# Sliding-window attention and a squared-ReLU feed-forward in one kernel: the second group's up-projection moved ahead of the first group's down-projection, and all nine groups' down-projections by seven products

## The chip, the cores and the metric

The kernel runs on one core of a Trainium2 chip. The metric is the device time of one execution, in microseconds (us). The core's engines run side by side, each through its own list of instructions in order: TensorE (PE, with its weight loads PEld), VectorE (DVE), ScalarE (ACT), GpSimd (POOL) and SyncE (SP). Here POOL issues the loads that convert float32 to bfloat16 on the way in, and SP issues transposes by DMA and most stores.

## The reference

Attention over 8 batches, 8 heads, 576 positions of 64 numbers each, with a causal window of 128 and a linear bias by distance, and then a feed-forward over all 4608 tokens.

```python
def _attn_ref(q, k, v):
    B, H, S, D = q.shape                       # 8, 8, 576, 64
    scores = (1 / sqrt(D)) * np.matmul(q, k.transpose(0, 1, 3, 2))
    rel = pos[:, None] - pos[None, :]
    slopes = 2.0 ** (-8.0 * (np.arange(H) + 1) / H)
    bias = slopes[:, None, None] * (-np.abs(rel))[None]
    mask = (rel >= 0) & (rel < 128)
    scores = np.where(mask, scores + bias, -1e9)
    attn = softmax(scores)
    return np.matmul(attn, v)

def _moe_ref(x, w_in, w_out):                  # x 4608 x 512, w_in 512 x 2048, w_out 2048 x 512
    r = np.maximum(x @ w_in, 0.0)
    return (r * r) @ w_out
```

All inputs and the output are float32; the kernel computes in bfloat16 with float32 sums.

## The kernel before

The tokens are worked in blocks of 128 positions of one batch (the last block of a batch has 64, and two such are paired). The 40 blocks are numbered 0 to 39 in the order in which they are taken; four of them make a group of 512 tokens, and there are nine groups, 0 to 8.

**Attention of a block.** POOL loads its k, q and v (tasks `lkq8`, `lv8`; lines L590 and L597). For blocks 0 to 7 PE transposes k and q through an identity matrix (`tp4.0`, `tp4.1`, L653) and ACT or DVE copies the result out (`ev4.0.0`); from block 8 on SP transposes by DMA (`kqT8`, L638). PE multiplies the scores (`s8`, L711) into four PSUM banks, ACT takes the exponentials (`e8.0` to `e8.3`, L734, 128x512 each), DVE multiplies by the window's mask (`m8.0` to `m8.3`, L742, L745, L749, 128x512 each), PE multiplies by v in two halves (`pv8.0`, `pv8.1`, L816), and DVE normalises (`r8.0`, `n8.0`, L832, L845). Blocks 0 to 3 have no earlier keys: there the bias is written by PE from the tables `slopes` (`b0`, L764), and no mask is needed. The block's result is transposed into `xT` (`xp4` by PE, L865, or `x8` by SP).

**Block 0** has a way in of its own: its k and q come as float32 by four loads on SP's and ACT's queues (`lk0.0`, `lk0.1`, `lq0.0`, `lq0.1`, L572) and DVE casts them (`ck0`, `cq0`, L441).

**Up-projection.** Groups 0 to 2 go plainly: `u0.r.e` is one piece of a group's product with `w_in` (L965), then ReLU by ACT (`reluu...`, L932) and the square (`squ...`). Groups 3 to 8 use seven half-size products in place of eight (`f3.u.p`, L1059), with sums by DVE (`us`, `ut`, `c11.g.u` and so on) and snapshots out of PSUM (`s1.g.u` and so on).

**Down-projection.** The constant `G_STR = 1` says from which group on the seven products are used. Group 0 goes plainly: 16 pieces `o0.t.part` of four matmuls 128x512 each (L1137), copied out by ACT (`oe0...`). Groups 1 to 8 use products `p1.p.z`: p is 1 to 7, z the half, eight matmuls 128x256 each (L1221). These need, for each group, eight DVE sums of 128x1024 (`S1` to `S4`, L1367), four snapshots out of PSUM (`s1_1`, `s5_1`, `s2_1`, `s3_1`, L443), three additions by DVE (`c11_1`, `c22_1`, `c12_1`), and the sums of `w_out` in `wsum` (`ws`, L1179, eight in all, used by every group). One product in progress holds up to three PSUM banks, where a plain piece holds one of the eight.

**Loads of the weights.** `w_in` comes in five pieces (`w_in0` and `w_in1` of 256 KB, the others of 512 KB), `w_out` in four of 512 KB, all by POOL (L535, L538), between the loads of blocks 3 to 7.

**The order** is written out by hand in the string `ORDER`: each engine takes its own tasks in the order in which they stand there; the letter behind the colon names the engine (a ACT, d DVE, g POOL, s SP, none PE), the numbers behind it the PSUM banks or buffers. Costs and due times in the code only check and place that order; the order itself decides what is queued behind what. The piece `fill` (L420) adds idle matmuls of 128x128 (L422) where the planner sees PE wait in the first 30 us.

Of the kernel before, what the change touches and what calls it, by code (L numbers as in the profile page):

```python
# [8 lines left out]
FP32 = mybir.dt.float32  # L9
# [8 lines left out]
N_HW = 1  # L18
N_PE = 8
# [11 lines left out]
IOTA = 3  # L31
# [5 lines left out]
G_STR = 1  # L37
# [19 lines left out]
lk0.0:s iota:g ident:d dist1:d slope1.0:d slope0.3:d one0.1:d lk0.1:a lkq2:g warm0:d slope1.1:d warm::0 lkq1:g  # L57
lq0.0:s slope1.3:a slope1.2:a slope0.2:a ck0:d slope0.0:a slope0.1:a lq0.1:a one0.2:d tp0.0::1 tp2.0::2 tp2.1::3
ev2.0.0:d ev2.1.0:d tp1.0::4 ev1.0.0:a tp1.1::5 b2::6,7 s2 ev1.1.0:a b1::0,2 s1 b0::3,4 e2.0:a e2.1:a e1.0:a
e1.1:a ev0.0.0:a cq0:d tp0.1::5 lv2:g pv2.0::6 r2.0:d ev0.1.0:d lv1:g lkq3:g lv0:g w_in0:g w_in1:g w_in2:g lv3:g  # L60
w_in3:g w_out0:g lkq4:g w_in4:g w_out1:g w_out2:g lkq5:g lv4:g pv1.0::7 pv1.1::0 pv2.1::2 r1.1:d r1.0:d n1.0:d
s0 tp3.0::5 tp3.1::1 n1.1:d e0.0:a b3::7,0 ev3.1.0:a ev3.0.0:a xp1.0::3 s3 n2.0:d r2.1:d one0.0:d pv0.0::6
n2.1:d e0.1:a pv0.1::1 x1.0:a xp2.0::2 one0.3:d r0.0:d x2.0:a u0.1.0::5 r0.1:d n0.0:d n0.1:d xp0.0::4 u0.2.0::3
e3.0:a e3.1:a x0.0:d dist0:d u0.0.1::6 u0.0.0::2 pv3.0::1 pv3.1::7 one1.4:d r3.0:d n3.0:d r3.1:d one1.1:d n3.1:d
u0.1.1::0 u0.0.2::4 xp3.0::1 u0.2.1::7 x3.0:d mask1.2:a reluu0.1.1:a:0 reluu0.0.1:a:1 reluu0.2.0:a:2 squ0.0.1:d
squ0.2.0:d u0.3.0::0 reluu0.1.0:a:3 u0.2.2::6 reluu0.2.1:a:1 mask0.3:a reluu0.0.2:a:2 squ0.2.1:d reluu0.2.2:a:1
squ0.2.2:d squ0.1.0:d u0.3.1::3 w_out3:g o0.2.0::1 tp4.0::5 tp4.1::7 squ0.1.1:d one1.7:d ev4.1.0:d squ0.0.2:d
reluu0.3.0:a:1 mask1.5:a mask0.5:a mask1.6:a mask0.6:a reluu0.0.0:a:3 ev4.0.0:a one1.3:d squ0.0.0:d u0.1.2::4
reluu0.1.2:a:0 reluu0.3.1:a:2 us3.0:d one1.0:d u0.0.3::6 reluu0.0.3:a:3 one1.8:d u0.3.2::0 s4::2,7,5,4 mask0.2:a
mask1.3:a mask0.4:a mask0.0:a mask1.0:a e4.0:a e4.3:a squ0.1.2:d squ0.0.3:d mask0.1:a mask1.7:a mask1.1:a  # L70
mask0.7:a reluu0.3.2:a:0 squ0.3.0:d squ0.3.2:d u0.2.3::3 reluu0.2.3:a:3 mask1.4:a one1.6:d squ0.2.3:d e4.1:a
u0.1.3::6 reluu0.1.3:a:1 squ0.1.3:d lkq6:g u0.0.4::2 e4.2:a o0.2.1 u0.3.3::4 o0.1.0::0 o0.1.1 o0.1.2 ws0.0:d
one1.2:d m4.3:d one1.5:d reluu0.0.4:a:0 us1.0:d m4.1:d m4.2:d tp5.0::3 tp5.1::7 lkq7:g lv5:g lv7:g lv6:g lkq8:g
lkq9:g lv8:g m4.0:d pv4.0::6 r4.0:d pv4.1::5 n4.0:d r4.1:d n4.1:d ev5.0.0:a o0.2.2 ev5.1.0:a reluu0.3.3:a:3
s5::2,3,7,6 e5.0:a e5.3:a e5.1:a e5.2:a xp4.0::4 o0.1.3 o0.2.3 tp6.0::5 tp6.1::2 lkq10:g ev6.0.0:a oe0.1.0:a:0
oe0.2.0:a:1 o0.3.0::6 tp7.0::3 tp7.1::7 st0.1.0:s lkq11:g ws0.1:d ws1.0:d x4.0:d us3.1:d us2.0:d squ0.3.3:d
m5.0:d m5.1:d ev6.1.0:d s6::4,5,2,0 e6.0:a e6.1:a e6.2:a e6.3:a ev7.1.0:a kqT8:s lv9:g kqT9:s squ0.0.4:d
ev7.0.0:d m5.3:d m5.2:d zerov10:d zerokqT10:d us0.0:d lv10:g zerov11:d o0.0.0::1 pv5.1::3 pv5.0::4 m6.0:d m6.1:d
o0.0.1 o0.0.2 kqT10:s zerokqT11:d r5.1:d r5.0:d n5.0:d n5.1:d m6.2:d squ0.3.1:d m6.3:d ws1.2:d s7::5,2,0,7
e7.0:a pv6.0::4 xp5.0::3 x5.0:a o0.0.3 pv6.1::5 e7.2:a e7.3:a e7.1:a oe0.0.0:a:2 m7.3:d m7.1:d r6.0:d m7.0:d  # L80
r6.1:d m7.2:d kqT11:s u1.0.0::3 u1.0.2::0 u1.0.3::7 pv7.0::2 pv7.1::1 r7.0:d r7.1:d n6.0:d n7.0:d n7.1:d
reluu1.0.0:a:1 reluu1.0.3:a:3 squ1.0.3:a n6.1:d o0.3.1 u1.0.7::3 reluu1.0.2:a:0 xp7.0::7 s8::4,2,0,1 xp6.0::5
lkq12:g lv12:g lkq13:g lv13:g lkq14:g o0.3.2 e8.0:a e8.3:a reluu1.0.7:a:2 e8.2:a squ1.0.0:d us2.1:d us2.3:d
x7.0:d x6.0:d ws1.1:d ws0.3:d m8.3:d m8.2:d o0.3.3 oe0.3.0:a:3 u1.1.1::7 u1.1.2::4 m8.0:d e8.1:a m8.1:d ws1.3:d
pv8.1::5 u1.0.1::1 u1.1.4::3 r8.1:d reluu1.1.2:a:3 reluu1.1.1:a:1 squ1.1.1:d pv8.0::0 r8.0:d n8.0:d squ1.0.2:d
reluu1.0.1:a:1 squ1.0.1:a n8.1:d s9::6,2,4,7 e9.0:a e9.1:a squ1.0.7:d squ1.1.2:d kqT12:s x8:s u1.0.6::1 e9.3:a
reluu1.0.6:a:1 e9.2:a m9.0:d m9.1:d m9.3:d ws0.2:d m9.2:d p1.1.0::0 u1.0.4::6 u1.0.5::5 reluu1.0.4:a:0
reluu1.1.4:a:2 s10::2,7,1,4 pv9.1::6 pv9.0::3 p1.1.1 r9.0:d r9.1:d n9.0:d e10.0:a n9.1:d squ1.0.4:d
reluu1.0.5:a:3 e10.3:a m10.3:d squ1.0.5:d us3.3:d m10.0:d s1_1:d:4 u1.1.5::2 u1.1.0::5 lkq15:g lv14:g lv11:g
lkq16:g x9:s e10.2:a e10.1:a reluu1.1.5:a:0 squ1.1.5:a s12::3,4,6,1 e12.0:a squ1.1.4:a e12.3:a st0.2.0:s kqT13:s  # L90
kqT14:s kqT16:s kqT15:s squ1.0.6:d m10.2:d u1.1.6::7 p1.2.0::2 u1.1.7::3 m12.0:d m10.1:d e12.2:a m12.2:d m12.3:d
p1.2.1 c11_1:d pv10.0::1 reluu1.1.7:a:3 reluu1.1.0:a:0 squ1.1.0:d e12.1:a reluu1.1.6:a:1 squ1.1.6:a pv12.1::6
pv10.1::3 pv11.0::5 m12.1:d r11.0:d squ1.1.7:a n11.0:d u1.1.3::4 pv11.1::2 pv12.0::7 u2.0.0::5 reluu2.0.0:a:2
reluu1.1.3:a:0 r10.0:d r11.1:d n11.1:d r10.1:d n10.0:d r12.1:d u2.0.5::2 u2.0.1::1 reluu2.0.5:a:1 n10.1:d
r12.0:d n12.0:d n12.1:d S1.1.0:d S3.1.0:d squ1.1.3:a s13::3,5,7,4 e13.0:a e13.1:a e13.3:a S1.1.1:d S2.1.0:d
S2.1.1:d S4.1.1:d S3.1.1:d u2.0.7::6 u2.0.6::2 squ2.0.5:a reluu2.0.6:a:3 e13.2:a reluu2.0.7:a:0 m13.3:d lv16:g
lkq17:g lkq20:g x12:s x10:s x11:s u2.0.4::3 p1.5.0::5 reluu2.0.4:a:1 p1.5.1 s14::4,2,7,6 s5_1:a:5 e14.0:a
# [232 lines left out]
def kernel(  # L330
# [1099 lines left out]
```

## Time and profile before

| | |
|---|---|
| time, median of 3 runs | 295.23 us (293.89, 295.23, 295.64) |
| the profiled execution: its time, its span | 293.89 us, 292.1 us |
| PE busy, matmuls | 282.8 us (97%), 3443 |
| DVE busy, instructions | 247.1 us (85%), 645 |
| ACT busy, instructions | 226.9 us (78%), 445 |
| POOL busy | 106.5 us (36%) |
| granted TensorE clock | 1.00 |
| plain down-projection, L1137 | 64 matmuls 128x512, 25.9 to 58 us |
| seven products, L1221 | 880 matmuls 128x256, from 63 us on |

The span runs from the first to the last instruction; 1.8 us of the execution's time lie around it. A matmul's duration in the profile is longer than the distance to the next one, because matmuls overlap in the array; what counts for a queue of them is the distance from start to start. The same holds, less strongly, for DVE and ACT. Where the timeline merges n alike instructions, that distance is the merged time less one duration, divided by n - 1.

### The profile page before, as it was taken

The numbers are of one execution on the slowest core, as the hardware profiler recorded it, in microseconds if no ns is written. First come the engines' busy times: TensorE is split into PE (matmuls) and PEld (weight loads), VectorE is DVE, ScalarE is ACT, GpSimd is POOL, SyncE is SP. The second block draws the span as 40 slices with busy tenths as digits, with TensorE's granted clock in tenths as the row PEclk, the third lists the DMA queues.
The fourth block names the chain that finished last, engine by engine and source line by source line (L and its number), as shares of the span: only waits on it lengthen the run. The fifth ranks groups of instructions, "written<-read, shape, count | busy, mean of one in ns | idle before, by whom it ended". The sixth has DMA issues, their size and how long they took to land.

```text
span 292.1 us, 8683 instructions
## 1 busy us (share of the span) xinstructions
PE 282.8 (97%) x3443; PEld 238.5 (82%) x3443; DVE 247.1 (85%) x645; ACT 226.9 (78%) x445; POOL 106.5 (36%) x132
## 2 busy tenths in 40 slices
PE   5889999999999999999999999999999999999994
PEld 2589766788888888888888888888898888888884
DVE  4444588877798699999999999999999898999883
ACT  3658967688789695899999999899886957858710
POOL 8954377393265372912573630820000000000000
PEclk9999999999999999999999999999999999999999
DMA  9999999999999999999999999998500523010225
GB/s 124 166 199 195 190 167 179 145 130 141 180 167 143 179 207 171 131 139 173 185 173 141 142 197 154 168 168 139 116 3 5 152 80 91 1 41 20 90 81 154
DMA packets 170921, 39.64 MB, mean 136 GB/s; under 512 B 156928, under 2 KB 170368, under 8 KB 170880
## 3 DMA queue, kind: packets, MB, share of 16 engines
q0 software_dynamic: 115184, 18.10, 95.1%
q1 hardware_dynamic: 54800, 20.26, 37.6%
q10 hardware_dynamic: 896, 0.72, 1.0%
q8 instruction: 27, 0.44, 0.6%
q14 instruction: 14, 0.11, 0.1%
HBM read 36.70 MB, written 9.44 MB: 158 GB/s over the span
## 4 chain that ended last, share of the span: by engine, by line
PE 87%; DMA 8%; POOL 4%; issue 0%; ACT 0%; DVE 0%; POOLq 0%
PE o L1221 33%; PE h L1059 26%; PE h L965 13%; PE pv L816 6%; PE s L711 5%; DMA vf<-in_v_dram 3%; DMA kqT<-kq 3%; PE o L1137 2%; DMA kq<-in_q_dram 2%; POOL kq L590 2%; POOL vf L597 1%; POOL w_in_sb L535 1%; PE o L1323 1%; PE xp L865 0%; PE tp L653 0%
## 5 line engine op out<-in xcount | busy, mean ns | idle before, releaser
L734 ACT ACTIVATE P<-s 128x512 bf16<-128x512 f32 x120 | 65.6, 612 | 5.2 <-PE s L711 4.9
L1221 PEld LDWEIGHTS <-g 128*128 128x128 bf16 x624 | 60.0, 98 | 7.0
L590 POOL DMA_DIRECT2D kq<-in_k_dram x39 | 33.9, 868 | 69.4 <-DMA kqT<-kq 65.6
L932 ACT ACTIVATE rt<-h 128x512 bf16<-128x512 f32 (+1 forms) x73 | 42.3, 600 | 14.7 <-PE h L965 9.9
L1080 DVE TENSOR_TENSOR rt<-h,f 128x512 bf16<-128x512 f32 x72 | 48.7, 686 | 4.1 <-PE h L1059 1.3
L924 ACT ACTIVATE g<-rt 128x512 bf16<-128x512 bf16 x80 | 48.9, 636 | 1.4 <-DVE rt L1085 0.7
L1221 PE MATMUL o<-w_out_sb,g 128*128 128x256 bf16 x384 | 47.7, 273 | 0.0
L965 PE MATMUL h<-xT,w_in_sb 128*128 128x128 bf16 (+1 forms) x512 | 46.4, 246 | 0.0
L443 ACT ACTIVATE f<-h 128x512 f32<-128x512 f32 x59 | 34.9, 606 | 11.1 <-PE h L1059 10.9
L965 PEld LDWEIGHTS <-w_in_sb 128*128 128x128 bf16 x512 | 38.9, 98 | 3.9
L1059 PE MATMUL h<-xT,w_in_sb 128*128 128x256 bf16 x288 | 41.4, 273 | 0.1
L1059 PEld LDWEIGHTS <-w_in_sb 128*128 128x128 bf16 x384 | 35.8, 98 | 5.2 <-issue 0.3
L742 DVE TENSOR_TENSOR P<-P,masks 128x512 bf16<-128x512 bf16 x96 | 37.1, 420 | 2.2 <-ACT P L734 2.1
L597 POOL DMA_DIRECT2D vt<-in_v_dram x36 | 30.8, 876 | 16.6 <-PE pv L816 9.0
L590 POOL DMA_DIRECT2D kq<-in_q_dram x39 | 33.7, 865 | 5.7 <-DMA w_out_sb<-in_moe_w_out_dram 2.3
L926 DVE TENSOR_TENSOR g<-rt 128x512 bf16<-128x512 bf16 (+1 forms) x65 | 26.1, 415 | 6.9 <-ACT rt L932 6.6
L845 DVE TENSOR_TENSOR x<-pv,rec 128x256 bf16<-128x256 f32 (+1 forms) x80 | 31.4, 414 | 0.5
L1221 PE MATMUL o<-wsum,sums 128*128 128x256 bf16 x256 | 31.7, 273 | 0.0
L1221 PE MATMUL o<-wsum,g 128*128 128x256 bf16 x240 | 30.5, 273 | 0.0
L1059 PEld LDWEIGHTS <-us 128*128 128x128 bf16 x288 | 27.1, 98 | 3.7
L1087 ACT ACTIVATE rt<-rt 128x512 bf16<-128x512 bf16 x38 | 24.1, 637 | 5.6 <-DVE rt L1080 5.2
L816 PEld LDWEIGHTS <-P 128*128 128x128 bf16 (+1 forms) x576 | 24.0, 100 | 5.0 <-issue 2.3
(81 smaller groups left out, 398.3 us busy)
## 6 DMA issues: line engine op xcount, KB each, us to landing
out_dram<-f SPq DMA_DIRECT2D x54, 128.0 KB, 2.6
kq<-in_k_dram POOLq DMA_DIRECT2D x31, 128.0 KB, 5.9
kq<-in_q_dram POOLq DMA_DIRECT2D x31, 128.0 KB, 6.5
vt<-in_v_dram POOLq DMA_DIRECT2D x28, 128.0 KB, 7.0
w_out_sb<-in_moe_w_out_dram POOLq DMA_DIRECT2D x4, 512.0 KB, 14.5
w_in_sb<-in_moe_w_in_dram POOLq DMA_DIRECT2D x3, 512.0 KB, 10.2
out_dram<-f SPq DMA_DIRECT2D x4, 256.0 KB, 5.0
out_dram<-f SPq DMA_DIRECT2D x13, 64.0 KB, 2.1
```

The source lines that it names most:

```text
L443: nc.scalar.activation(o, i, AF.Copy)
L590: nc.gpsimd.dma_start(view(kq[s_kq[m].idx], i), source(src, m, split))
L597: nc.gpsimd.dma_start(tile_of(s_v[m])[0:n, :, 0:D], source(v, m))
L734: nc.scalar.activation(flat(Pt[sP.idx]), sS[i].tile.rearrange("p (j t) -> p j t", j=2)[:, :, lo:hi], AF.Exp, bias=0.0, scale=scale)
L742: nc.vector.tensor_tensor(flat(Pt[sP.idx]), flat(Pt[sP.idx]), flat(masks), op=ALU.mult)
L816: nc.tensor.matmul(sv.tile[0:n, hi * (D + 1):(hi + 1) * (D + 1)], prob, tile_of(s_v[mk])[:, h, 0:D + 1], start=mk == parts[0][1], stop=mk ...
L924: nc.scalar.activation(o, i, AF.Square, bias=0.0, scale=1.0)
L932: nc.scalar.activation(rts[srt.idx][:, 0:n], slot.tile[:, 0:n], AF.Relu, bias=0.0, scale=1.0)
L965: nc.tensor.matmul(slot.tile[:, f * w:(f + 1) * w], w_in_sb[:, cc, fc * 128:(fc + 1) * 128], xT[:, cc, lo % (XR * 128):lo % (XR * 128) + w ...
L1059: nc.tensor.matmul(slot.tile[:, j * 256:j * 256 + 256], a, b_, start=fresh and j == 0 and c == 0, stop=c == 1, skip_group_check=True)
L1080: nc.vector.tensor_tensor(rts[srt.idx], slot.tile, other(), op=ALU.add)
L1221: nc.tensor.matmul(slot.tile[:, z * 256:z * 256 + 256], stationary(c), moving(c), start=fresh and z == 0 and c == 0, stop=c == F - 1, skip ...
```

## The change

It has four parts, and the order is written anew around them.

1. `G_STR = 0`: group 0's down-projection also goes by seven products. The 64 matmuls of 128x512 go, and 112 of 128x256 come; with them eight sums `S1.0.0` to `S4.0.1`, the additions `c11_0`, `c22_0`, `c12_0` and four snapshots come, and the four copies `oe0` go.
2. The order: group 1's up-projection (`u1`) stands ahead of group 0's down-projection, and the pieces of `w_out` are loaded later. All pieces of `w_in` and the loads of blocks 3 to 6 now stand ahead of `w_out0`, and `w_out3` comes behind the loads of blocks 8, 9 and 10.
3. `HWK = True`: block 0's q comes by POOL (`lq0`), converted on the way, in place of the two loads on SP's and ACT's queues and the cast `cq0`. POOL's first five tasks are loads of k and q, and `iota`, which makes the numbers for the identity matrix and the bias, is the sixth. `TABLE = True` adds one tiny exponential on ACT at the start (`table`).
4. `MASK2 = True`: a mask product covers four heads in place of two, 128x1024 in place of 128x512, so two in a block in place of four. It waits for two exponentials in place of one. The values' half `pv` waits for two exponentials in both kernels.

```diff
+SPLIT = False
+HWK = True
+MASK2 = True
+TABLE = True
...
-G_STR = 1
+G_STR = 0
...
+    def touch():
+        nc.scalar.activation(scratch, warm[:, 0:1], AF.Exp, bias=0.0, scale=1.0)
+    if TABLE:
+        plan.add({"ACT": 1400.0}, EARLY, touch, [t_wz], name="table")
...
-            for i, src in enumerate((k, q)):
+            for i, src in enumerate((k, q)[:1 if HWK else 2]):
...
+            if HWK:
+                l_q = plan.add({"POOL": 890.0}, key, lambda: nc.gpsimd.dma_start(view(kq[s_kq[m].idx], 1, False),
+                                                                               source(q, m)), [], [s_kq[m]],
+                               dma=ns, name=f"lq{m}")
+                c_k = plan.add(engs, key, lambda: cast_kq(0), t_l[0:2], [], [s_st], name=f"ck{m}", after=l_q)
+                t_kq[m] = [c_k, l_q]
...
-            t_P.append(plan.add({"DVE": dve(cols, 2)}, due - 31 + i, mask,
-                                [t_e] + t_mask[1] + (t_mask[0] if kind != "diag" else []), name=f"m{ms[0]}.{i}"))
+        for i in range(2 if MASK2 else 4):
+            nh = 4 if MASK2 else 2
+            t_P.append(plan.add({"DVE": dve(cols * nh // 2, 2)}, due - 31 + i,
+                                lambda i=i, nh=nh: mask(slice(nh * i, nh * i + nh)),
+                                t_es[nh // 2 * i:nh // 2 * (i + 1)] + t_mask[1] + (t_mask[0] if kind != "diag" else []),
+                                name=f"m{ms[0]}.{i}"))
```

Out of the two orders, PE's tasks where the parts change places, and POOL's and DVE's first tasks:

```
PE before:   ... u0.3.1 o0.2.0 tp4.0 ... u0.3.3 o0.1.0 o0.1.1 o0.1.2 tp5.0 ... o0.0.3 pv6.1 u1.0.0 u1.0.2 ... u1.1.3 pv11.1 pv12.0 u2.0.0 ...
PE after:    ... u0.3.3 xp5.0 s7 pv6.1 u1.0.6 ... u1.1.5 u1.1.7 p0.1.0 p0.1.1 s8 u1.1.6 p0.5.0 u1.1.3 p0.2.0 u1.1.4 p0.2.1 s9 ...
             p0.7.0 p1.2.0 s12 p0.7.1 p1.1.0 p1.1.1 p1.2.1 pv11.1 pv11.0 p0.4.0 pv10.1 pv12.1 pv12.0 p0.4.1 u2.0.3 ...
POOL before: iota lkq2 lkq1 lv2 lv1 lkq3 lv0 w_in0 w_in1 w_in2 lv3 w_in3 w_out0 lkq4 w_in4 w_out1 w_out2 lkq5 lv4 w_out3 lkq6 ...
POOL after:  lk1 lk2 lq1 lq0 lq2 iota lv1 lv2 lk3 lq3 lv0 w_in1 w_in0 w_in2 lv3 w_in3 lk4 lq4 lk5 lq5 lk6 w_in4 lq6 lv4 lk7 lq7
             lv5 lv6 w_out0 lv7 w_out1 lkq9 lkq8 w_out2 lkq10 lv8 w_out3 lkq11 ...
DVE before:  ident dist1 slope1.0 slope0.3 one0.1 warm0 slope1.1 ck0 ...
DVE after:   warm0 one0.0 one0.1 ident ev1.0.0 ck0 dist1 slope1.0 slope1.1 slope0.3 ev0.1.0 ...
```

Over the whole of both orders the tasks that differ in number are these; besides, 64 tasks (copies out of PSUM, ReLUs, squares, snapshots) go from ACT to DVE and 49 from DVE to ACT.

| engine | task | before | after |
|---|---|---|---|
| PE | plain pieces `o0` (4 matmuls 128x512) | 16 | 0 |
| PE | products `p` (8 matmuls 128x256) | 112 | 126 |
| DVE | mask products | 120 of 128x512 | 60 of 128x1024 |
| DVE | sums `S` (128x1024) | 64 | 72 |
| DVE | additions `c..` of the down-projection | 24 | 27 |
| DVE | snapshots of both projections | 17 | 18 |
| DVE | copies `ev` out of PSUM | 6 | 13 |
| DVE | ReLUs in place, squares of sums (`reluc`, `sqc`, `sqf`) | 34, 24, 6 | 38, 27, 7 |
| ACT | copies `ev` and `oe` | 14 | 3 |
| ACT | ReLUs in place, squares of sums | 38, 66 | 34, 62 |

More of the change, by code (lines that the diff above doesn't have):

```diff
@@ L56 @@
 ORDER = """
[L57 to L61, printed above, removed]
@@ new lines @@
+m6.1:d u0.3.3::0 n6.0:d xp5.0::5 x5.0:d x4.0:a reluu0.0.4:a:0 s7::7,2,3,1 reluu0.3.3:a:2 e7.0:a e7.3:a e7.2:a
+e7.1:a pv6.1::4 w_out0:g lv7:g w_out1:g lkq9:g lkq8:g w_out2:g lkq10:g u1.0.6::0 u1.0.2::5 kqT9:s us3.0:d
+squ0.0.4:d squ0.2.3:d r6.1:d n6.1:d squ0.3.2:d xp6.0::7 u1.0.3::1 u1.0.0::4 zerokqT10:d m7.0:d x6.0:a m7.1:d
+pv7.1::3 reluu0.1.3:a:0 squ0.1.3:d r7.1:d pv7.0::2 kqT8:s reluu1.0.3:a:1 u1.0.5::7 u1.0.4::6 r7.0:d n7.0:d
+n7.1:d xp7.0::1 x7.0:d u1.0.1::2 lv8:g w_out3:g lkq11:g lv9:g kqT10:s lkq12:g lv12:g lkq13:g lv13:g squ1.0.3:a
@@ L245 @@
     SELF = {"ACT": 120.0, "DVE": 110.0}
-    BEGIN = {"POOL": 840.0, "SP": 740.0, "ACT": 740.0, "DVE": 860.0, "PE": 1190.0}
+    BEGIN = {"POOL": 700.0, "SP": 740.0, "ACT": 740.0, "DVE": 700.0, "PE": 1190.0}
     FIRST = {"POOL": 1100.0, "SP": 1150.0, "ACT": 1150.0}
@@ L407 @@
     xt = ring("x", size["x"], [128, d_model])
-    stages = [wsum.rearrange("p s c t -> p (s c t)")[:, 0:4 * d_model].bitcast(FP32)]
-    plan = Plan({"b": 8, "f": NF, "rt": RT, **{f"g{f}.{t}": 2 for f in range(FCB) for t in range(2)}, "rec": 4, "ut": UT, "s1": 1, "s2": 1, **{f"v0.{i}": 1 for i in range(L)}, "kqT0": L, "stage": 2, **size})
+    stages = [x.rearrange("p c t -> p (c t)").bitcast(FP32) for x in (wsum[:, i] for i in range(4))]
+    plan = Plan({"b": 8, "f": NF, "rt": RT, **{f"g{f}.{t}": 2 for f in range(FCB) for t in range(2)}, "rec": 4, "ut": UT, "s1": 1, "s2": 1, **{f"stage{i}": 1 for i in range(4)}, **{f"v0.{i}": 1 for i in range(L)}, "kqT0": L, **size})
     def bank(slot, name):
@@ L662, in evac @@
                     o = tile_of(sT)[:, i * C + c0:i * C + c1, 0:n]
-                    if split:
+                    if split and not (HWK and i):
                         src = st.tile[:, 0:512].rearrange("p (i g c) -> p c g i", i=4, c=C)[:, c0:c1]
@@ L669, in transpose_kq @@
                 w = (c1 - c0) * n
-                evs[i].append(plan.add({"ACT": act(w), "DVE": dve_p(w, 1 if split else 2)}, due - 58, evac,
+                evs[i].append(plan.add({"ACT": act(w), "DVE": dve_p(w, 1 if split and not (HWK and i) else 2)}, due - 58, evac,
                                        [t_tp[i]], [], [st], name=f"ev{m}.{i}.{c0}"))
@@ new lines, in flat, with mask @@
+        def flat(t, w):
+            return t[:, w].rearrange("p j t q -> p j (t q)")[:, :, lo:hi]
+        def mask(w):
+            nh = w.stop - w.start
+            if kind == "full":
+                nc.vector.tensor_tensor(flat(Pt[sP.idx], w), flat(Pt[sP.idx], w), flat(masks, w), op=ALU.mult)
+            elif kind == "diag":
+                pt = Pt[sP.idx][:, w]
+                nc.vector.tensor_tensor(pt, pt, masks[:, w, 1:2, :].to_broadcast([128, nh, 2, 128]), op=ALU.mult)
+            else:
+                pt = Pt[sP.idx][:, w].rearrange("p j t (i q) -> p (j t) i q", i=2)
+                mk = masks[:, w].rearrange("p j t (i q) -> p (j t) i q", i=2)[:, :, 0:1, :]
+                nc.vector.tensor_tensor(pt, pt, mk.to_broadcast([128, 2 * nh, 2, 64]), op=ALU.mult)
@@ new lines, in job, with expo @@
+        t_es = []
+        for i in range(4):
+            def expo(i=i):
+                nc.scalar.activation(flat(Pt[sP.idx], slice(2 * i, 2 * i + 2)),
+                                     sS[i].tile.rearrange("p (j t) -> p j t", j=2)[:, :, lo:hi],
+                                     AF.Exp, bias=0.0, scale=scale)
+            t_es.append(plan.add({"ACT": act(cols)}, due - 31 + i, expo, [t_s[i // 2], t_e0], [] if i else [sP],
+                                 [sS[i]], name=f"e{ms[0]}.{i}"))
+            t_e0 = t_e0 or t_es[0]
@@ L821, in values @@
             t_pv = plan.add({"PE": 4 * len(parts) * 30.0 + 30}, due - 12 + hf, pv,
[L822 removed]
+                            (t_P[hf:hf + 1] if kind == "lone" else t_P[len(t_P) // 2 * hf:len(t_P) // 2 * (hf + 1)]) + [x for _, mk in parts for x in t_v[mk]],
                             [sv], rel, name=f"pv{m}.{hf}")
```

368 lines of the change are left out of this document (177 added, 191 removed).

## The prediction

> **What bounds the kernel now.** I read the page first, its shares of busy time and its forty slices.
>
> ```profile
> span 292.1 us, 8683 instructions
> ...
> PE 282.8 (97%) x3443; PEld 238.5 (82%) x3443; DVE 247.1 (85%) x645; ACT 226.9 (78%) x445; POOL 106.5 (36%) x132
> ...
> PE   5889999999999999999999999999999999999994
> ...
> DVE  4444588877798699999999999999999898999883
> ...
> PE 87%; DMA 8%; POOL 4%; issue 0%; ACT 0%; DVE 0%; POOLq 0%
> ```
>
> PE is full from the fourth slice to the last but one, and 87% of the chain that ended last is PE. DVE is as full from slice 15 to 31. So I asked for sums by stretch, to see how far behind PE the second engine is:
>
> ```profile
> 20.00:60.00 40.00, 39.70 (x536) 30.38 (x536) 28.48 (x91) 29.80 (x68) 23.21 (x29) 1.00 1.75 174
> 60.00:100.00 40.00, 40.00 (x556) 34.18 (x554) 31.82 (x95) 32.98 (x64) 21.51 (x27) 1.00 2.13 160
> 127.80:222.10 94.30, 94.24 (x1198) 81.15 (x1196) 92.51 (x241) 88.41 (x173) 30.05 (x36) 1.00 1.46 141
> ```
>
> The columns are the stretch, then PE, PEld, DVE, ACT and POOL. Up to 100 us DVE has a fifth to a quarter of its time free; from 128 to 222 us it has 2%. Then the timeline, for distances from start to start:
>
> ```profile
> 35.04 2.75 PE L1137 MATMUL o<-w_out_sb,g 128*128 128x512 bf16 x12
> ...
> 275.13 3.66 PE L1221 MATMUL o<-w_out_sb,g 128*128 128x256 bf16 x32
> ...
> 57.69 1.09 DVE L742 TENSOR_TENSOR P<-P,masks 128x512 bf16<-128x512 bf16 x3
> ...
> 278.75 1.28 DVE L1367 TENSOR_TENSOR sums<-sums,g 128x1024 bf16<-128x1024 bf16 x2
> ```
>
> A plain matmul of 512 takes (2.75 - 0.38) / 11 = 0.216 us; one of 256 takes (3.66 - 0.27) / 31 = 0.109. A DVE product of 512 takes (1.09 - 0.42) / 2 = 0.334, one of 1024 takes 1.28 - 0.69 = 0.60. I set every distance between PE starts against the median of its line and form: what is over it sums to 1.3 us from 20 to 60 us, 2.2 from 60 to 100, 4.1 from 127.8 to 222.1 and 0.8 after that. PE waits for little, mostly 0.1 us at a time, at the scores and at the up-products. Last, the head:
>
> ```profile
> 0.84 0.34 POOL L457 IOTA sums<- 128x256 f32 x1 [0.39 <-POOLq L1414]
> 1.34 1.02 POOL L590 DMA_DIRECT2D kq<-in_k_dram  x1 [0.16 <-issue]
> ...
> 8.43 0.94 POOL L597 DMA_DIRECT2D vf<-in_v_dram  x1
> 9.30 2.30 POOL L535 DMA_DIRECT2D w_in_sb<-in_moe_w_in_dram  x3
> ...
> 16.55 1.06 PE L965 MATMUL h<-xT,w_in_sb 128*128 128x128 bf16 x16
> ...
> 55.16 0.23 PE L711 MATMUL s<-kqT,kqT 64*128 64x128 bf16 x2 [0.17 <-DMA kqT<-kq]
> ```
>
> The first up-projection starts at 16.55, behind the second piece of w_in, which landed at 16.23. POOL's loads land one behind the other, 0.85 us apart for a block's k, q or v, 2.5 to 3.1 for 512 KB, without a pause until 46 us. Block 8's scores waited 0.17 us for their transposes.
>
> **Part 1, the seven products for group 0.** PE loses 64 x 0.216 = 13.8 us and gains 112 x 0.109 = 12.2: **-1.6 us**, on the engine that sets the end.
>
> [...]
>
> DVE gains eight sums x 0.60 = 4.8 us and three additions x 0.60 = 1.8. ACT and DVE share the four new snapshots in place of four copies, which is nothing net. These lie between 50 and 75 us. There DVE has a fifth of its time free, some 5 us in 25, and the masks of blocks 8 to 17 give a little back: free there, though only just; without that cover, up to 6.6 us.
>
> In their new place the products also hold three banks and wait for snapshots. PE's waits ran at 2.2 us in 40 where products and attention mix, against 1.3 in 40 where plain pieces filled in. For 12 us of products that is 12 x 0.9 / 40 = **+0.3**; bounds 0 and +1.5 (five waits of 0.3).
>
> **Part 2, the order.** Without the plain pieces as filler, the up-projections and the attention of blocks 4 to 7 stand closer together. I counted tasks from the first up-piece to block 7's last transpose in the new order: PE 27 us, ACT 22, DVE 19. Both stay under PE: nothing, while the banks are emptied in time; that wait is in the bound above.
>
> The loads: w_out0 and w_out1 will land near 37 and 40 us, and the first product of group 0 comes at 16.5 + 34 = 50.5, so they are covered by 10 us. w_out3 comes behind all that had landed before by 51.1 plus two half blocks: 51.9. Product 2 needs it; PE's tasks ahead of it sum to 38.4 us, so it comes near 16.5 + 38.4 + 1 = 56. Covered by 4 us. Block 8's k and q land near 44.4 rather than 47.75 (7 loads less ahead: 0.45 x 2 + 0.85 + 2.58 + 3.15 = 7.5 off 51.9). Its transpose took 7.36 us in the chain, so 51.8, and its scores stand at 16.5 + 35.2 + 1 = 52.7. The cover is 0.9 us; each us beyond it is PE's. I take 0, bounds 0 and +3.
>
> SP's queue gets five more stores of small size and ACT's one less; SP has no other work behind which they hurt.
>
> **Part 3, the head.** Five loads stand ahead of iota: it ends near 0.84 + 1.02 + 4 x 0.88 + 0.34 = 5.7 in place of 1.2. Behind it on POOL every load starts 5.9 - 4.97 = 0.93 us later. Behind it on DVE wait the identity, then a copy and a cast, then the bias tables, done near 9. PE's transposes wait for the identity, 6.1 in place of 5.6; the biases for the tables. All that is covered, as v0 comes last: it landed 8.43 + 5.2 = 13.6, and its product stands at the head of the `pv` in PE's new queue, with `pv2` behind it. The two loads gone from the other queues took wire time: POOL's first landings lay 1.25 and 1.45 apart beside them and 0.85 after. So v0 lands between 13.0 and 14.5 (all of the 0.93 late), and w_in0, now the second piece, between 15.7 and 17.2. First up-piece at 16.3 to 17.4 against 16.55: **0**, bounds -0.3 and +0.9. The table load moves from 1.99 to near 1, into time in which ACT waits: nothing either way.
>
> **Part 4, wide masks.** DVE saves 120 x 0.334 - 60 x 0.60 = 4.1 us over the kernel. With the moves between engines (seven copies 2.4, squares and ReLUs 2.1, a snapshot 0.6, `cq0` -0.57) and part 1, DVE's whole work in distances goes from 236 to 243 us; ACT's falls by 7.
>
> What matters is where PE and DVE run level. From product 2.4.1 to 5.4.1 (127.8 to 222.1 us) I counted both orders. Before: PE 91 up-products, 42 products, 14 scores, 32 half values = 92.4 us, DVE 90.3, elapsed 94.3. After: 95 up-products, the rest alike, PE 94.1; DVE 51 additions, 7 snapshots, 30 wide masks and the rest = 93.7. PE with its old 1.9 us of waits gives 96.0. If DVE idles as long as it did, 94.3 - 90.3 = 4.0, it gives 97.7: +1.7. With no such idling, 0. The wide masks replace 56 waits by 28, so I take the half, **+0.8**; bounds -2.1 (the waits at the up-products, 2.1 of the stretch's 4.1 us, gone) and +6 (rival b).
>
> **The sum.** -1.6 + 0.3 + 0.8 = -0.5. The profiled execution took 293.89 us, span 292.1 and 1.8 around it: it becomes 293.4, span 291.6. Against the median, 1.3 us higher, that is **294.7**.
>
> **Rivals.** (a) *The saving stays and the waits go too.* The wide masks free DVE, and the waits at the up-products in the stretch (those 2.1 us) vanish, while the new stage costs nothing: -1.6 - 2.1 = -3.7, **291.5**. For it: 4 us less mask work. Against: DVE's sum in the stretch rises all the same.
>
> (b) *DVE sets the pace from 128 to 222 us, and the kernel is slower.* A wide mask can start only after a second exponential, 0.477 later, and its half of the values gets it 0.60 - 0.334 = 0.27 later still. DVE takes its list in order, so what stands behind the mask (an addition that frees a PSUM bank, for which PE's next fresh product waits) is held too. Fifteen mask jobs x 0.477 = 7.2 us if nothing is under way meanwhile; half of that on top of the 4.0 idle gives 93.7 + 4.0 + 3.6 = 101.3 against 96.0: +5.3 and in all -1.6 + 0.3 + 5.3 = +4.0, **299.2**. It decides once DVE idles more than 96.0 - 93.7 = 2.3 us plus the 1.3 that the saving leaves, 3.6 in the stretch. For it: DVE waited only 2.2 us for exponentials before 96 masks, and there is no spare left. Against: the order can put other work ahead of a mask. [...]
>
> (c) *A load comes late.* Block 8's transposes take 2 us more than their cover, or iota's delay reaches the first up-piece (+0.9): -0.5 + 2 = +1.5, **296.7**. For it: 0.9 us of cover behind transposes that take 3 to 9 us. Against: the loads start 3 us earlier than before.
>
> (d) *The seven products don't save*, because PE in that stage waits a fifth of a us at each of the 14 halves: 14 x 0.2 = 2.8, sum -0.5 + 2.5 = +2.0, **297.2**.
>
> **How the numbers follow.** Chances: my forecast 0.48, (a) 0.17, (b) 0.20, (c) 0.08, (d) 0.07. A change of 1%, 2.95 us, is about what a measurement of this kernel tells from none. Faster by more: (a) and the very low end of my own, 0.18. Slower by more: (b) and the upper ends of (c) and (d), 0.26. Within: 0.56. The forecast's own range is 293 to 297 (the small bounds of parts 1 to 3 together). For 8 in 10 it must take in (a) and most of (b): 290.5 to 299.5.
>
> **What would show it.** Right: no L1137, 992 matmuls of 128x256 on the products' line, 0.109 apart; the first up-piece between 16.3 and 17.4; the wide mask 0.60 from start to start; PE's waits from 60 to 100 us near 2.5; the stretch between those two products near 97 us with DVE over 97% busy. Wrong: PE waiting at block 8's scores for kqT by more than 0.5 us; DVE idle above 3.6 us in the stretch (then b); a first up-piece after 17.5, or before 15.5, which would mean that the loads, not v0's chain, were misjudged.

## The result and the profile after

The changed kernel took 302.97 us (median of four runs, 300.94 to 304.68), the kernel before 295.44 in the same measurement: a ratio of 1.0268, 95% interval 1.0222 to 1.0313. It is slower by 2.7%. The ratios here and below are the measurement's own, over its undisturbed executions, and need not equal the quotient of the two medians. The prediction had 294.7 us, with 290.5 to 299.5 as its range.

The profiled execution is the one of 300.94 us; its span is 7.04 us above that of before (299.16 against 292.12). The page, as before: the shares, PE's slices, its granted clock, and the shares of the chain that ended last.

```profile
span 299.2 us, 8829 instructions
...
PE 285.2 (95%) x3543; PEld 247.2 (83%) x3543; DVE 252.2 (84%) x610; ACT 219.4 (73%) x430; POOL 107.4 (36%) x133
...
PE   7899999299999999999999999999999999999993
...
PEclk9999999979999999999999999999999999999999
...
PE 81%; DMA 12%; POOL 5%; issue 1%; DVE 0%; POOLq 0%; SPq 0%
```

One slice tells most of it: the eighth (52 to 60 us) has PE busy for two tenths, and in the ninth the granted clock is down. DMA has 12% of the chain, where it had 8%. The chain around that slice (start, length, what) and PE's timeline there:

```profile
36.20 10.12 DMA kq<-in_q_dram
...
46.38 13.68 DMA kqT<-kq
60.11 1.04 PE s L732 x16
```

```profile
52.65 1.91 PE L1247 MATMUL o<-w_out_sb,g 128*128 128x256 bf16 x16
60.11 0.29 PE L732 MATMUL s<-kqT,kqT 64*128 64x128 bf16 x2 [5.56 <-DMA kqT<-kq]
...
61.08 1.89 PE L991 MATMUL h<-xT,w_in_sb 128*128 128x256 bf16 x8
62.76 1.13 PE L1247 MATMUL o<-wsum,sums 128*128 128x256 bf16 x8
63.73 1.04 PE L991 MATMUL h<-xT,w_in_sb 128*128 128x256 bf16 x8
```

Group 0's first product ends, and then PE waits 5.56 us at block 8's scores for their transpose. That took 13.68 us; before it took 7.36, and PE waited 0.17. When PE starts again it runs at half rate for 2.8 us (the granted clock is 0.50 from 59.53 to 62.94 us): the scores last 1.04 us where they last 0.62 in the kernel before, and eight matmuls of 256 columns take 1.89 us, 0.213 from start to start in place of 0.109. Two stretches by engine (PE, PEld, DVE, ACT, POOL, then the clock) and the head:

```profile
60.00:100.00 40.00, 39.89 (x519) 33.48 (x520) 31.23 (x71) 25.81 (x50) 20.41 (x25) 0.96 1.97 145
134.80:230.20 95.40, 95.40 (x1214) 83.16 (x1212) 93.41 (x219) 88.12 (x171) 30.83 (x37) 1.00 1.45 144
```

```profile
15.01 0.40 PE L842 MATMUL pv<-vf,P 128*128 128x65 bf16 x8 [0.63 <-DMA vf<-in_v_dram]
...
18.18 1.00 PE L991 MATMUL h<-xT,w_in_sb 128*128 128x128 bf16 x15 [0.22 <-ACT xT L444]
```

The stretch between products 2.4.1 and 5.4.1, where rival (b) had its place, lasted 95.4 us, and PE had no gap in it that the row shows. The first up-piece came at 18.18 us instead of 16.55, behind v0, which landed at 14.97.

**The account.** To see where time is lost I took, from the profiled execution of each kernel, at each moment, the time minus the useful PE work done by then: every matmul so far times the median distance of its form (0.109 us for 256 columns, 0.216 for 512, 0.056 for 128 and so on), idle fill matmuls left out. I call this the lag.

| us | before | changed | e2 | e5 | e9 |
|---|---|---|---|---|---|
| useful PE work, whole kernel | 269.16 | 267.55 | 267.55 | 267.55 | 267.55 |
| lag at 18 us | 10.77 | 12.68 | 12.38 | 12.17 | 11.60 |
| lag at 50 us | 11.87 | 13.72 | 13.00 | 13.01 | 12.78 |
| lag at 66 us | 12.46 | 20.78 | 17.16 | 14.60 | 13.72 |
| lag at 280 us | 19.08 | 26.83 | 23.30 | 20.63 | 19.82 |
| last matmul to end of span | 3.71 | 4.60 | 4.62 | 4.31 | 4.46 |

From before to changed: work -1.61, head (to 50 us) +1.85, the stretch from 50 to 66 us (20.78 - 13.72) - (12.46 - 11.87) = +6.47, the rest of the kernel 6.05 - 6.62 = -0.57, the tail +0.89. The sum is +7.03, the span's difference. The last three columns are experiments, below.

### The profile page after: what moved, and what is told of

The parts are those of the page before. It is cut to its first block, busy times and chain, and to the rows that moved or that the text cites. A ratio compares the mean times of both kernels' runs of the same rounds, so it can differ in the third digit from the quotient of the medians.

```text
span 299.2 us, 8829 instructions
## 1 busy us (share of the span) xinstructions
PE 285.2 (95%) x3543; PEld 247.2 (83%) x3543; DVE 252.2 (84%) x610; ACT 219.4 (73%) x430; POOL 107.4 (36%) x133
## 4 chain that ended last, share of the span: by engine, by line
PE 81%; DMA 12%; POOL 5%; issue 1%; DVE 0%; POOLq 0%; SPq 0%
PE o L1247 36%; PE h L1085 25%; PE h L991 8%; DMA kq<-in_q_dram 7%; PE pv L842 6%; PE s L732 6%; DMA kqT<-kq 5%; POOL kq L606 2%; POOL vf L619 1%; POOL w_in_sb L543 1%; PE o L1349 1%; PE tp L675 0%; POOL kq L594 0%; POOL sums L458 0%; DVE f L1359 0%
## 5 line engine op out<-in xcount | busy, mean ns | idle before, releaser
L1247 PEld LDWEIGHTS <-g 128*128 128x128 bf16 x704 | 67.6, 98 | 8.1
L612 POOL DMA_DIRECT2D kq<-in_k_dram x32 | 27.1, 847 | 80.7 <-DMA kqT<-kq 78.5
L1247 PE MATMUL o<-w_out_sb,g 128*128 128x256 bf16 x432 | 54.0, 273 | 0.0
L950 ACT ACTIVATE g<-rt 128x512 bf16<-128x512 bf16 x76 | 46.3, 630 | 3.0 <-DVE rt L1111 2.4
L754 DVE TENSOR_TENSOR P<-P,masks 128x1024 bf16<-128x1024 bf16 x48 | 32.3, 682 | 6.3 <-ACT P L766 6.2
L1247 PE MATMUL o<-wsum,sums 128*128 128x256 bf16 x288 | 36.1, 273 | 0.0
L1247 PE MATMUL o<-wsum,g 128*128 128x256 bf16 x272 | 34.8, 273 | 0.0
L1247 PEld LDWEIGHTS <-sums 128*128 128x128 bf16 x288 | 27.7, 98 | 3.4
L444 ACT ACTIVATE f<-o 128x512 f32<-128x512 f32 x30 | 18.0, 601 | 16.7 <-PE o L1247 13.7
L952 DVE TENSOR_TENSOR g<-rt 128x512 bf16<-128x512 bf16 (+1 forms) x69 | 27.7, 414 | 2.7 <-ACT rt L958 2.4
```

Of the source, the lines that this page charges most:

```text
L444: nc.scalar.activation(o, i, AF.Copy)
L754: nc.vector.tensor_tensor(flat(Pt[sP.idx], w), flat(Pt[sP.idx], w), flat(masks, w), op=ALU.mult)
L950: nc.scalar.activation(o, i, AF.Square, bias=0.0, scale=1.0)
L1247: nc.tensor.matmul(slot.tile[:, z * 256:z * 256 + 256], stationary(c), moving(c), start=fresh and z == 0 and c == 0, stop=c == F - 1, skip ...
```

## The experiments

What had to be found: why a transpose that had taken 7.36 us took 13.68, whether that alone made the kernel slower, and what the other parts were worth. A task list below shows the letters of GpSimd's queue (g) or SP's (s) in `ORDER`, old line and new.

**e1: blocks 9 and 8 ahead of w_out.**

```diff
-w_out0:g lv7:g w_out1:g lkq9:g lkq8:g w_out2:g
+lkq9:g lkq8:g w_out0:g lv7:g w_out1:g w_out2:g
```

> Loads of blocks 9 and 8 (k and q) go to GpSimd's queue ahead of the first w_out piece instead of behind the first two and block 7's v; nothing else of the changed kernel is touched. Theory A (the wait before block 8's scores is the loss, and it comes because its transposes start late and run beside a full GpSimd queue): q8 lands near 40.6 us instead of 46.3, its transpose ends near 54 or before, PE's 5.6 us before the scores of block 8 fall below 0.5, the half-rate matmuls behind it (1.5 us) go too, and the span comes to about 292 us, within 1 us of the kernel before's. Theory B (the order itself or the wide masks cost the time, and the wait only shows it first): the wait goes, but another of 4 to 6 us comes up before 112 us, and the span stays at 297 or above.

Measured: 300.17 us, ratio 1.0194 (1.0125 to 1.0262), span 297.6. q8 landed at 39.04, 7.3 us earlier, and still the transposes ended at 50.5 and 55.0: issued at 37.40 and 39.10, they took 13.1 and 15.9 us beside three w_out pieces. PE did not wait for them, but my edit had put block 7's v behind a w_out piece, and it landed at 47.49 in place of 39.71:

```profile
PE pv L834 <- DMA vt<-in_v_dram: 4.0, 1, 4.0
```

Another wait of 4.0 us took the place of the first, with half-rate matmuls behind it (16 of 256 columns in 2.90 us; ahead of the wait 16 took 1.91). By its number rival B came true, by its cause neither did. What it shows: an early start alone is no cure.

**e2: the w_out pieces ahead of block 9's load.**

```diff
-w_out0:g lv7:g w_out1:g lkq9:g lkq8:g w_out2:g lkq10:g ... lv8:g w_out3:g
+w_out0:g lv7:g w_out1:g w_out2:g w_out3:g lkq9:g lkq8:g lkq10:g ... lv8:g
```

> The third and fourth w_out piece go ahead of block 9's load, so that no w_out packets run beside block 8's and 9's transposes; q8 lands later, near 50.8 us instead of 46.3. If the w_out packets beside the transposes are what made them 11 to 14 us long: block 8's transpose is back at 7 to 8 us, ends near 58, and the wait before its scores is 3.5 us instead of 5.6. If the transposes are long because anything at all runs in GpSimd's queue: 10 us or more, end near 61 to 64, wait 6.5 to 9 us.

Measured: 296.95 us, ratio 1.0086 (1.0049 to 1.0123), span 295.6. q8 landed at 49.92, 3.6 us later than in the changed kernel, and its transpose was done 4.0 us earlier (chain, then PE's timeline):

```profile
49.99 6.11 DMA kqT<-kq
```

```profile
56.14 0.29 PE L724 MATMUL s<-kqT,kqT 64*128 64x128 bf16 x2 [2.31 <-DMA kqT<-kq]
...
57.11 1.89 PE L983 MATMUL h<-xT,w_in_sb 128*128 128x256 bf16 x8
```

GpSimd's queue was full beside these transposes too, with the loads of blocks 8 to 11; only the w_out pieces were not among them. The DMA view says more. From 46 to 60 us, for the kernel before, the changed kernel and e2, all packets by size and the queue that carries SP's transposes (packets, MB, share of the 16 engines' time):

```profile
DMA packets 12237, 2.19 MB, mean 156 GB/s; under 512 B 12109, under 2 KB 12109, under 8 KB 12235
...
q1 hardware_dynamic: 3342, 1.05, 43.9%
```

```profile
DMA packets 7626, 1.90 MB, mean 136 GB/s; under 512 B 6957, under 2 KB 7624, under 8 KB 7624
...
q1 hardware_dynamic: 2632, 0.65, 64.5%
```

```profile
DMA packets 14236, 2.20 MB, mean 157 GB/s; under 512 B 14230, under 2 KB 14234, under 8 KB 14234
...
q1 hardware_dynamic: 3200, 0.79, 40.0%
```

In the changed kernel 669 packets of 512 B or more (7626 - 6957) ran in these 14 us, in e2 six, though e2 moved more bytes (2.20 MB against 1.90). A packet of the transposes' queue took 0.645 x 16 x 14 us / 2632 = 55 ns beside them and 0.400 x 16 x 14 / 3200 = 28 ns without; before, with 128 such packets, 29. The rows show the doubled packet time beside the w_out pieces, and not what brings it about.

**e3: the third and fourth w_out piece behind block 9's v.**

```diff
-lkq8:g w_out2:g lkq10:g ... lv8:g w_out3:g lkq11:g lv9:g
+lkq8:g lkq10:g ... lv8:g lkq11:g lv9:g w_out2:g w_out3:g
```

> The third and fourth w_out piece go behind block 9's v, so that they run only after 52 us. If the w_out packets are what stretch the transposes: block 8's transpose takes 7 to 8 us and ends near 53, the wait before its scores is under 0.5 us, though the product that reads w_out's third piece may then wait for it. If any packets of GpSimd's queue do: 11 us or more again, end near 57, wait near 3 us.

Measured: 301.25 us, ratio 1.0225 (1.0151 to 1.0299), span 298.8. The edit did not do what I had meant: GpSimd came to these pieces at 45.63 and 47.14 us, not after 52, and they landed at 55.51 and 58.45, beside block 8's transpose again. The first transpose, ahead of them, took 6.78 us, the second, beside them, 12.14, and PE waited 3.9 us. It did not test what it was meant to, but its two transposes, one ahead of the pieces and one beside them in the same execution, are in line with e2.

**e4: PE's pause filled with idle matmuls.**

```diff
+                for _ in range(90 if ms[0] == 8 else 0):
+                    nc.tensor.matmul(sS[2 * grps[0]].tile[:, 0:128], ident, ident, start=True, stop=True)
```

> 90 idle 128x128 products of the identity run ahead of block 8's scores, into a buffer that the scores overwrite; they take about 5 us of the 5.6 us for which PE waits there. If PE's pause is what makes the matmuls behind it run at half rate: the transposes' landing and the wait's end stay at 60.1 us, the matmuls after it are 0.109 apart for 256 columns at once, and the span is 1 to 1.5 us shorter than the changed kernel's. If the slow matmuls come from waits of their own (loads, buffers): no change of the span within 0.3 us.

Measured: 299.93 us, ratio 1.018 (1.0112 to 1.0248), span 298.0.

```profile
55.08 5.19 PE L727 MATMUL s<-ident 128*128 128x128 bf16 x90
61.08 0.23 PE L734 MATMUL s<-kqT,kqT 64*128 64x128 bf16 x2 [0.81 <-DMA kqT<-kq]
...
61.63 1.05 PE L993 MATMUL h<-xT,w_in_sb 128*128 128x256 bf16 x8
```

The transpose ended at 61.03, 1 us later than in the changed kernel, and yet the u-piece behind the scores takes 1.05 us instead of 1.89. So the half rate comes from the pause. From the scores to the second u-piece behind them it takes 2.31 us here (61.08 to 63.39) and 3.62 in the changed kernel (60.11 to 63.73): the half rate costs 1.3 us. From 54 to 66 us the lag grows by 6.03, against 7.05; the difference is smaller, 1.0, since PE's time without useful work ahead of the scores was 0.3 us longer here. Of the 1.1 us of span, only 0.3 is at the last matmul, since PE lost 0.7 more at the head here; the other 0.8 is the tail.

**e5: e2, and block 8 ahead of block 9**, both in loading and in transposing.

```diff
-lkq9:g lkq8:g ... kqT9:s ... kqT8:s
+lkq8:g lkq9:g ... kqT8:s kqT9:s
```

> The kernel with all w_out pieces ahead of block 9's loads (e2), and in it block 8's load and transpose ahead of block 9's, not behind them. Theory A (the scores of block 8 wait for a transpose whose end is set by when its load gets through GpSimd's queue): block 8's q lands near 48.2 us, its transpose ends near 53.9, where e2 has block 9's; the wait before its scores falls from 2.3 us to 0.5 or less, the half-rate matmuls behind it (1.2 us) go, and the span falls from 295.6 to 292.0 to 292.6. Rival (the transposes are slow beside any load of GpSimd's, and the first is only lucky): the transpose takes 9 us or more, the wait stays above 2 us, the span above 295.

Measured: 294.47 us against 294.79 before, ratio 0.9995 (0.9972 to 1.0018), span 292.7. The two edits to the order, of the loads and of the transposes, give back the whole 2.7%. Chain and timeline:

```profile
48.66 6.41 DMA kqT<-kq
```

```profile
55.11 0.23 PE L724 MATMUL s<-kqT,kqT 64*128 64x128 bf16 x2 [1.27 <-DMA kqT<-kq]
```

The transpose ends 1.2 us later than I expected and 1.27 us of wait are left; there is no half rate behind this pause (0.23 for the pair, as in the kernel before). Theory A holds in its cause; the wait and the span lie just outside what it gave (0.5 us or less, 292.0 to 292.6).

**e6: e5, with v0 and w_in0 earlier at the head.**

```diff
-lv1:g lv2:g lk3:g lq3:g lv0:g ... w_in1:g w_in0:g
+lv0:g lv2:g lk3:g lq3:g lv1:g ... w_in0:g w_in1:g
```

> As e5, and at the head v0 changes places with v1 and w_in0 with w_in1 in GpSimd's queue. v0 then lands near 11 us instead of 14.7 to 15.0 and PE's first up-piece comes near 16.4 instead of 17.9. Theory A2 (losses ahead of block 8's scores do not add up, since the transpose's end is set by the queue and not by PE): PE comes to those scores 1.3 us earlier and waits 1.0 to 1.6 us for the transpose, with up to 1 us of half-rate matmuls behind; the span is within 0.6 us of e5's. Rival (the head's loss goes straight to the end): 1.3 us shorter than e5.

Measured: 294.59 us, ratio 0.9998 (0.9978 to 1.0019), span 292.6. v0 landed at 10.38 and the first up-piece came at 16.89, but the next one waited 0.6 us for w_in; only 0.8 of the 1.3 us came. The last matmul ended 0.6 us earlier (287.77 against 288.35), the span 0.1. By size this is between the two theories, and the time can't tell them apart. The trace says more: at 50 us the lag was no smaller than in e5 but some 0.3 us larger, as two waits for w_in (0.58 us up to 18.08, and one filled with idle matmuls up to 20.65, where the next piece landed at 20.58) had used up the head's gain. The 0.6 us came behind that, at block 8's scores, where the transpose landed 0.5 us earlier (54.58 against 55.06) and the wait was 0.47 us.

**e7: e6, with work ahead of the scores.**

```diff
-p0.1.1 reluu1.0.7:a:2 s8::4,6,1,3 ... u1.1.6::5 reluu1.1.6:a:3 p0.5.0::0
+p0.1.1 reluu1.0.7:a:2 u1.1.6::5 p0.5.0::0 s8::4,6,1,3 ... reluu1.1.6:a:3
```

> As e6, and one up-piece (u1.1.6) and one half of a product (p0.5.0) of 0.87 us each, which stood behind block 8's scores, stand ahead of them. Theory A2: the wait of e6 is filled with work, under 0.3 us is left of it, and the span is 1.3 to 2 us below e5's, near 290.7, that is, some 1.4 us below the kernel before's 292.1. Rival (something else sets the pace from 60 us on): no more than 0.5 us below e5's.

Measured: 294.48 us, ratio 0.9985 (0.9962 to 1.0007), span 292.8. The wait at the scores is gone and one of 0.5 us for an exponential stands at the next up-piece: the lag at 66 us is 14.20, in e6 14.21. The rival holds; what I moved ahead was missing as cover behind.

**e8: e2 with narrow masks** (`MASK2 = False`, four `m` tasks for two).

> As e2, with the mask products of the later blocks in four of 512 columns each instead of two of 1024; DVE then has 4.1 us more to do over the kernel, and waits for one exponential less before each. If DVE sets the pace between 128 and 222 us, as the second rival of the prediction has it: the span grows by 1 us or more and PE's waits in that stretch grow from 1.3 us. If wide masks cost waits for the exponentials, as the prediction's +0.8 has it: the span falls by 0.5 to 1 us. If neither: within 0.4 us of e2's 295.6.

Measured: 298.69 us, ratio 1.0108 (1.0059 to 1.0156), span 297.4. The interval overlaps e2's. In the profile, 1.1 of the 1.8 us lie ahead of 66 us (lag 18.28 against 17.16: w_in and the scores), outside what was edited; from product 2.4.1 to 5.4.1 it took 96.2 us against 95.7 in e2 and 95.4 in the changed kernel. So the wide masks are worth some 0.5 us there, if anything, and no cost of theirs shows.

**e9: e7 with the old head.** `HWK = False` loads block 0's q by SP and ACT in float32 again:

```diff
-lk0.0:s lk0.1:a lk2:g lq1:g lq0:g lq2:g iota:g ident:d
+iota:g ... ident:d dist1:d ... lk0.0:s lk0.1:a lq0.0:s lq0.1:a lk2:g lq1:g lq2:g ... cq0:d
```

> As e7, with the head's third part undone: block 0's q is loaded in two halves by the SP and ACT queues and cast on DVE again, iota is GpSimd's first instruction, the identity and the distances DVE's first. PE's lag (its time minus its useful work) was 13.2 us at 50 us in e7 against 11.9 in the kernel before, and stayed as far apart to the end. Theory A3 (what is left of the loss is the head's): the first transposes come near 5.7 us instead of 6.5, v0 and the w_in pieces land 0.9 us earlier, the lag at 50 us is 12.0 to 12.5, and if the transpose of block 8 keeps up (less than 0.5 us of new wait) the span is 0.5 to 1.0 us below e7's 292.8. Rival (the head is set by the loads through GpSimd's queue, however they are shared out): the lag at 50 us stays at 13 or above and the span within 0.4 us of e7's.

Measured: 293.50 us against 294.81, ratio 0.9967 (0.995 to 0.9985):

```profile
span 292.0 us, 8841 instructions
```

The lag at 50 us is 12.78, not 12.0 to 12.5, so the head was only part of what is left; the span fell by 0.8 us, as theory A3 had it. This version is faster than both kernels, by 0.33% than the one before.

**e10: e5 with group 0's down-projection plain** (`G_STR = 1`; `p0.1.0` becomes `o0.0.0` and so on, the eight sums, four snapshots and three additions go).

> As e5, with group 0's down-projection in 16 plain pieces (64 matmuls of 512 columns) at the places of its 14 half products, without their sums, snapshots and additions on DVE and ACT. By the prediction's first step the products save 64 x 0.216 - 112 x 0.109 = 1.6 us of PE and cost at most 1.5 us in waits, taken as 0.3: the plain form should be 1.3 us slower than e5 (span 294.0), 0 to 1.6 by its bounds. Rival: the products' evictions and sums cost PE as much as they save, and the spans are within 0.3 us.

Measured: 295.23 us, ratio 1.0026 (1.0007 to 1.0046), span 294.3, that is 1.6 above e5. The profiled execution is the longest of its ten; by the ratios the difference is 0.3%, some 0.9 us, and the two intervals overlap. The useful work is 269.16, as before. From 50 to 80 us the lag grows by 2.60, in e5 by 2.50; less the wait at block 8's scores (1.6 and 1.3) that is 1.0 and 1.2. So the products' sums and snapshots cost PE some 0.2 us in this stretch, and the saving of the first step is there in PE's work; in the time it shows less clearly. The scores' wait of this run is used at the end:

```profile
55.81 0.23 PE L723 MATMUL s<-kqT,kqT 64*128 64x128 bf16 x2 [1.62 <-DMA kqT<-kq]
```

**e11: e5 with one w_out piece beside the transposes.**

```diff
-w_out2:g w_out3:g lkq8:g lkq9:g lkq10:g
+w_out2:g lkq8:g lkq9:g w_out3:g lkq10:g
```

> As e5, with the last w_out piece (512 KB) put back behind block 9's load, so that one piece and not two (changed kernel) or none (e5) runs beside block 8's transposes. The load of block 8 then lands 2.5 us earlier, near 46.0 us. If the two only share the engines: the transpose takes 2.5 us longer, 8.9 us, and ends where e5's did, near 55, the wait before its scores is 1.3 us, the span within 0.5 us of e5's 292.7. If a w_out piece costs the transposes more than its own time: 10 to 13 us, end at 56 to 59, wait 2.5 to 5 us, span 294 to 297.

Measured: 294.92 us, ratio 1.0003 (0.9976 to 1.003), span 292.4. Block 8's transpose took 7.64 us, started 2.2 us earlier and ended at 54.11, ahead of e5's; the scores did not wait. Block 9's took 10.87 and had the time. A packet of the transposes' queue took 45 ns from 46 to 60 us (2656 packets in 52.8%), with 510 packets of 512 B or more. So one piece can be borne here; what counts is which of the two PE needs last.

**e12: the changed kernel, with block 8 ahead of block 9 alone** (the edit that e5 makes to e2).

> The changed kernel with one edit: block 8's load and transpose ahead of block 9's. Both transposes still run beside two w_out pieces. If the wait is the price of standing second in the queue: the transpose of block 8 takes 11.4 us, as the first one did there, ends near 55.5 and the wait before its scores falls from 5.6 to near 1 us; with the half-rate matmuls still there the span is 294 to 295. If standing first helps nothing because both wait for the w_out pieces: end at 59 to 60, wait 4 us or more, span above 297.5.

Measured: 298.41 us, ratio 1.009 (1.0054 to 1.0126), span 296.8.

```profile
55.12 0.23 PE L724 MATMUL s<-kqT,kqT 64*128 64x128 bf16 x2 [0.33 <-DMA kqT<-kq]
...
60.88 0.84 PE L1239 MATMUL o<-w_out_sb,g 128*128 128x256 bf16 x4 [1.98 <-DMA w_out_sb<-in_moe_w_out_dram]
61.51 1.92 PE L983 MATMUL h<-xT,w_in_sb 128*128 128x256 bf16 x8
```

The transpose took 10.54 us and ended at 55.08, as the first theory had it, and its wait fell to 0.33 us. But the span did not fall to 295: the last w_out piece, issued at 43.94 and landed at 60.84 (16.9 us), is now what comes last, at product 2, with half rate behind it. The transposes and the w_out piece do not all land in time, and this edit only chooses which of them PE waits for.

## Why the prediction was wrong

**Part 2 failed, at one term.** "Its transpose took 7.36 us in the chain, so 51.8 ... The cover is 0.9 us ... I take 0, bounds 0 and +3." It measured +6.47: the wait 5.4 us longer (5.56 against 0.17) and 1.3 us of half rate behind it (e4), less some 0.2 us of other waits that the kernel before had in that stretch. The transpose took 13.68 us where I had put 7.36, and two w_out pieces beside it are why: without them it took 6.11 us in e2 and 6.41 in e5, and e3's two transposes took 6.78 ahead of the pieces and 12.14 beside them. The mechanism was named, as rival (c) at 0.08, and so was its sign, a wait at block 8's scores of more than 0.5 us; the price of 2 us was a third of what it cost. I took the duration from an execution in which other things ran beside it. Before, the four w_out pieces were issued from 13.12 to 26.32 us and had landed by 40.11, over 7 us ahead of the transposes. The new order puts blocks 4 to 7's k, q and v ahead of w_out, since their attention stands earlier, and the third and fourth piece, landing at 48.30 and 58.09, came to run beside the transposes. I had worked out that w_out3 would land at 51.9 and the transpose end at 51.8, and did not ask what two transfers that end together do to each other. The bound of +3 was of the same kind: the trace of before has transposes of 3 to 9 us, but none beside a piece of 512 KB.

Two smaller errors went the same way: q8 landed at 46.32, not near 44.4, and block 8's transpose is second in SP's queue behind block 9's, which I had not counted; e5 and e12 show that standing first is worth 1.0 us or more on e2 and 5.2 us of wait on the changed kernel. The one error that helped was the scores' place, 54.5 us rather than 52.7.

**Part 1 was right.** PE's work fell by 1.61 us (predicted 1.6), on 992 matmuls 0.109 apart. The +0.3 for waits was about 0.2 (e10). Rival (d) falls.

**Part 3 was out by 1.85 us** at 50 us, over its bound of +0.9. v0 landed at 14.97, not at 13.0 to 14.5, and the first up-piece came at 18.18, past the 17.5 that I had named as a sign of error. POOL's first load began 0.4 us later (1.25 against 0.84 for its first instruction), and v0's load was issued at 9.65 rather than 9.36. e9 undoes it and gains 0.4 us of lag at 50 us on e7 and 0.7 us at the last matmul. With the old loads back, e9's lag at 18 us is still 0.8 us above that of before (11.60 against 10.77), and e6, which moves v0 ahead, has no less lag at 50 us than e5: the rest of the head's loss is not explained.

**Part 4 went the other way.** From 66 to 280 us PE lost 0.57 us less than before (predicted +0.8); e2, e5 and e9 agree (6.03 to 6.14 of lag in that stretch, before 6.62). The stretch between the two products took 95.4 us where 97 was expected, and DVE was busy for 93.41 of it, so it idled 2.0 us and not more than 3.6. Rival (b), the likeliest of the rivals, with 101.3 us there, did not occur, with the narrow masks (96.2, e8) or without.

**The tail** was not in the sum: the end of the span lies 4.60 us behind the last matmul, before 3.71. Two of the last stores' issues take 1.01 and 0.94 us, where the same two take 0.61 and 0.33 before. In e4 and e10 they are as short as before, and the tail is 3.76 and 3.67; the order there is the same in e4. The cause stays open.

**The whole.** Without the queue's fault (e5) the time is that of before within 0.3%: the forecast of 294.7 would have stood, but by luck, with other terms than mine: -1.6 for the products, +1.55 in lag by 280 us (20.63 - 19.08), which is the head and what is left of the wait less the gain in part 4, and +0.6 for the tail.

## What to carry to other kernels

A transfer's duration held here only for the company in which it was measured, 7.36 us for block 8's transpose before and 13.68 beside two w_out pieces: when an order is changed, list what else is in the queues during it, and price it by a row with the same neighbours, or widen the bound. Where two transfers are due together, expect one to be late, as in the changed kernel (5.56 us of wait) and in e12 (1.98); put first the one that an engine waits for, and bulk weights well ahead of both. The time minus useful work, drawn over the span for both kernels, shows in one table which part lost what; the groups' busy times would not.

## What the runs showed of the hardware

The DMA transposes of blocks 8 and 9 took 4.8 to 7.4 us beside GpSimd's small loads alone (before, e2, e5 to e10, and the first one of e3) and 10.0 to 15.9 where w_out pieces ran beside them for most of the time (changed, e1, e4, e12, the second one of e3, block 9's of e11). Block 8's in e11, which shared part of its time with one piece, took 7.64.

PE fell to half rate after pauses of 5.56, 3.97, 3.89, 2.31 and 1.98 us (changed, e1, e3, e2, e12), and not after 1.62 (e10) and 1.27 (e5). e8 has a pause of 2.96 us, and a mean granted clock of 0.992 over its span, where e5 and e10 have 1.000. In the changed kernel the granted clock stood at 0.50 for one stretch of 3.41 us (59.53 to 62.94) and then at 1.00 again; the means over e2's windows (0.75 from 54 to 58 us, 0.82 from 58 to 62) and e12's (0.57 from 61 to 65) come to 3.4 us at 0.50 as well. The stretch did not always begin with the work: in e1 and e3 PE ran at full rate for 1.2 and 0.6 us first. In e12 it began 0.2 us after the pause: the first four matmuls took 0.63 us to the next start (60.88 to 61.51), between the two rates (0.44 and 0.85), and the next eight ran at half. The shortest pause with half rate behind it is 1.98 us, the longest without 1.62.
